# A residual block on one Trainium2 core: the same instructions in another order

## The chip, the core and the metric

The kernel runs on one core of a Trainium2 chip. A core has four compute engines with a queue of instructions each: TensorE (PE, matrix products; its weight loads are shown as PEld), VectorE (DVE), ScalarE (ACT) and GpSimd (POOL). SyncE (SP) issues most DMA transfers, POOL the rest. Each engine works through its own queue in order; between engines, semaphores say when an operand is ready or a buffer is free. The metric is the device time of one execution in microseconds (us), lower is better.

## The reference

```
B, C, HW, E = 2, 512, 64, 1152
def gn(z, gamma, beta):              # group norm, 4 groups, eps 1e-5
    zr = z.reshape(B, G, (C // G) * H * W)
    mu = zr.mean(-1).reshape(B, G, 1)
    var = ((zr - mu) ** 2).mean(-1).reshape(B, G, 1)
    zn = ((zr - mu) / jnp.sqrt(var + eps)).reshape(B, C, H, W)
    return zn * gamma.reshape(1, C, 1, 1) + beta.reshape(1, C, 1, 1)
def conv3(z, w):                     # 3x3 convolution, zero padding, 512 to 512 channels
    zp = jnp.pad(z, ((0, 0), (0, 0), (1, 1), (1, 1)))
    taps = [jnp.einsum("bchw,oc->bohw", zp[:, :, i:i+H, j:j+W], w[:, :, i, j]) for i in range(3) for j in range(3)]
    ...
h = conv3(_silu(gn(x, g1, be1)), w1)
emb = _silu(t_emb) @ w_emb
h = h + emb.reshape(B, C, 1, 1)
h = conv3(_silu(gn(h, g2, be2)), w2)
return x + h
```

Two images of 512 channels and 64 x 64 points pass through two 3x3 convolutions, each behind a group norm and a SiLU, with an embedding added between them and the input added at the end. Inputs and output are bfloat16.

## The kernel before

The work is cut into eight **chunks** c = 0 to 7: layer (0 to 3 the first convolution, 4 to 7 the second), image, and half of the image's rows. In each chunk there are four **units** k = 0 to 3, one for each 128 output channels. The four tiles of 128 input channels are called ct. One partition holds one channel.

The convolution is not computed as nine products. VectorE and ScalarE first combine the rows of the input (and, in the later chunks, its columns) into a few sums, so that fewer products are needed; TensorE multiplies these with combined weights; then the products are combined back into output rows. Per chunk and input tile, `prod(c, ct)` does the first part: `load_a` loads a slab of x or of the stored intermediate h_scr, `silu` applies the norm's scale and shift and the SiLU on ScalarE, `rows_a` and `rows_b` make the row combinations, mostly on VectorE. Per chunk and output tile, `unit(c, k)` does the rest: groups of matmuls into PSUM banks, an evacuation of each bank by ScalarE, and then additions on VectorE that give the output rows in a buffer `ys`. `prod(c+1, k)` is written into the program next to `unit(c, k)`, so VectorE prepares the next chunk while TensorE multiplies this one.

Weights are prepared as well: `prep_w1` combines the first layer's weights on VectorE with scaling passes on ScalarE (128x1536), `prep_w2` does so for the second layer piece by piece (two loads and two 128x384 scaling passes for each of 16 pieces, called w2_jc below), stores them to DRAM, and `fetch_w2` brings them back in chunk 3. `stats0` and `stats1` compute the first norm's statistics, `gn2` the second's. `emb` multiplies the embedding in five short groups of products. At the start TensorE runs 11 + 8 filler products with a matrix of ones ("warm", "fill").

Names in the text are those that the code gives its operations. u63y is unit 3 of chunk 6, the addition "y" that completes the rows; u63m0 is an evacuation of that unit; silu22, k22, row22, rob22 belong to chunk 2 and input tile 2. "k" is a multiplication by 4 of the slab (line 352 on VectorE, 371 on ScalarE), "row" and "rob" are additions (line 348).

**What sets the order.** The code is written as a plan: every operation is recorded in a list, 2,753 of them (1,208 groups of products for TensorE, 821 VectorE, 428 ScalarE, 33 POOL, 263 DMAs), each with its reads and writes in one large SBUF buffer `ar` (addresses fixed by hand) and in PSUM. From these the plan derives which operation must follow which. At the end `emit` issues them in the order that a string, ORDER, spells out: two characters for each operation, a number in base 64.

```
seq = [64 * al.index(order[i]) + al.index(order[i + 1]) for i in range(0, len(order), 2)]
assert sorted(seq) == list(range(len(self.ops)))
done = set()
for i in seq:
    assert all(p in done for p in self.ops[i].preds)
    done.add(i)
    self.ops[i].fn()
```

So ORDER is the only thing that decides how operations stand behind each other in the five queues (PE, DVE, ACT, POOL, SP). Each helper records its operations on one line: additions on VectorE at line 348 (`tt`), multiplications at 352 (`ts`), everything on ScalarE at 371 (`act`), DMAs at 386 (`dma`), products at 401 (`mm`), clearing on POOL at 390. In the profile, lines therefore tell the kind of an operation, and its place in time tells which it is.

Buffers are shared tightly. The two buffers for second-layer weights (RAW) lie in memory that the statistics of the second image use before; an operation that overwrites a buffer waits for its last reader, whichever engine that is on.

Of the kernel before, what the change touches and what calls it, by code (L numbers as in the profile page):

```python
# [115 lines left out]
def _idx(off, dims):  # L116
# [49 lines left out]


ORDER = (
    "0D0E0F0G0H0I0R0S0T0U0W2T1u0v0y1Q2J1N2c3F1r2M0c0X0a0Z0Y0d0e0f00010b020g13030h14150i0j0k0l0L0m170n0N16180405061907"
    "081X1Y1Z1A1_0o1a1c0K1B0M1C1D0p0O1E1b1F1d0q0r1e0s1f0_1g1G1H2021231I1h090A0B0V0C3K1i0J22240t0u0w250x0z1j1J2610271k"  # L170
    "2e12281K292U1l2A1T2B1m1n112C1o2D1x2E2F1U2G1y2P1z1-1W0-1L1M1O1P1R1S1p1q1s1t1v1w2H2I2K2L2N2O3C3D3E3L0Q2Q1V2R2S0P3M"
    "4g2W2l2X2m2Y2n3G2Z4T3g4L2f3O2i3P3N3Q2h3S3R2g3V2a3H3a3W3U2o2p3h3i2q2r2s2t2u2v2w2x2y2z3j2-3u4M2d2j4N2k2_304U2b3Z32"
    "314O5P3X3k3c3d3b5H3Y3T4h4P5I4Q5J4k4V334X4W4Y344Z35364b374a3e4S4R3f384d4m4e4n4f6Y4j3v3w3x3y3z3-3_4243443l45464748"
    "494q4r4s4t3m41404B5Q4A6L4i4c5K6D5L5M6F6M6E4u4v3n3o4w4x4-4_50515253543p555c5d5e5f5h2V4l6Z5R3r6a5T7u5U5S5V3q5W5X7v"
    "5Z5a4p3s5N4C3t3I4D4G4F4E7w4H5b8y4o3J56395Y6GB7B84I3A4z574y3B6IB96H5g586N596P5B5C6O5A6Q5D6RBB6T6SBABD6U6K6W6J6X8z"
    "5O6V5i5j5k5l5m5n5o5r5s5t5u5w5x5y5z5-5_60616b6c6d6e6g5v5q5p6h6i6j6k6l6m6n6s6t6u6v6x6y6z6-6_70717262767763BC4JBN7h"
    "BF6fBP4KBH648-65A0686766BJA169A2BR5E8lBOBGBED56A5F6w7P78797A6o7B7C7D7x7y7z7-5G6p8081BQ828384858687BI74737EDDB47Q"
    "6q7RB57S6r7T7UB67V757W7XBL7FD7DF7YBK7ZBS7aBT7b7G7c7d7H7e7K7f7J7g7i8988D66BDEBM7ID97LDH7j7l8A7m7k7n8B7o7pD27tDL7M"
    "BUEeDN8C8D8EDG7_8F8H8I8J8K8L8M8N8O8S8T8U8V8W8X8Y8Z8_908GD88Q8P91929495969798999A9B9G9H9I9J9L9M9N9O9P9Q9R9S8a9W9X"
    "8m8b7O9p9q6CD37r8RD4DIDB7sDA8cDJ7N7q8d8n8f8p8o8q8g8r8e9C9D8t8s8hDP8v9KEgDKDMDC93DOEfEh9UAt9FEi9EDRDQ9T8x8w9V9Y9Z"  # L180
    "9a9b9c9d9f9eA3A4A5A6A8A9AAABACADAEAFAKALAMANAPAQARASATAUAVAWAaAbAcAdAeAfAgAhEm8u9r9t9s9u9v9w9x8iEuEo9gEjAG9hEqEn"
    "GB9yCrEwA7EpAHAuAO8kEk9k9j9-9i9_9l9zAXCsAYAiAjAvAIAxAwAyAJAzA-A_AZB0B2B3AkCQAlAoAnAmCRCtEvDSEl8jApEO9m9nAqCvB1Cw"
    "CuCxCTCyCzBVBWBXBYBaBbBcBdBZBiGDBjBeBfBgBhBlBmBnBoBtBuBvBwByBzB-B_C0C1C2C3C6C7C8C9CCCDCECFDTDUDVDW9oBkDYDZDaDbBp"
    "BqExBsEbEyEcCUBrEdE-EsErBxEPC5C4AsCAGJCGD0CVCSEzCWCBD1CHC_CIDcDdDeDfDjDkDlCXCYDmDrDsDtDuDwDXDhGLDgDxDyDzD-D_E0E1"
    "E4E5E6E7EAEBECEDF0F1F2F3FxEtE_GCGKDiCKCLG8CJC-G9GFGNCMCZGAArGRCaEQGEESERETGHEUGGEWEVDnDoDvGTGMFyE8E2E3EEGPDpDqCb"
    "EYE9GVHhHUHVGSHjGIEFEJEaCcEGEZEHGOCNCOEXHpHiGQGUF5F6F7F8F9FAFBFCFGFHFIFJFOFPFQFRFTFUFVFWFXFYFDEIGXHlCdGWEKCeFzFE"
    "FKFLF4HrFFHkHxHzFbFZFaFdFcFeFfFgFhFjFkFlFmGZGaGbGcGeGfGgGhGiGjGkGlFSGpGqGrGsGxGyGzG-H0H1H2H3FnH4H5H6H7HqGYHsCPF_"
    "CfG0F-G1CgG3G2ChFMFNCiHtCjFiCkG5FoHvClFpCmG7HmFqFsGmI3FrGuGoGtGnI5J6ELJ7G4HuHnFtG6HyHoI7GvHWKNGdHAHBHCHDHGHHHIHJ"
    "IBICH8ENH9FuI4EMHYHXHZH_HaCnCpHbCoHcGwCqHdHgHfHEG_HFHeHKI6KPJ8J9HwH-KONMNLFvHLIDIEIGIHIIIJIKILIMINIRISITIUIZIaIb"
    "IPIOIFIcIeIfIgIhIiIjIkIlIoIpIqIrIuIvIwIxIQJSJTJUJVJXJYJZJaI8HMIWHPHOIVI0HNI1I9JAHQIXIYImInIsJCJBJDJEItJFJGJJKQIy"  # L190
    "IdIzJHKRI-JKJIJ1IALeLfI2HRJLLgFwMvJ0KTI_KUKSJ2KVKWKXJMNJMwMxHSJWJgJfJbJcJdJeJiJjJkJlJqJrJsJtJmJhO-OzJvJwJxJyJzJ-"
    "J_K0K3JnNKK1K4K5K6K9KAKBKCKjKkKlKmKoKpKqKrKsKtKuKvKzK-K_L0JuK2KbKYLhLiJpJ3KaKZJNJoK7HTKDJ4QBQAOkJOLjLkJPLlLmK8Lo"
    "KELnKnKFKIKGKHLqLpKJKxL1KyKwMyL2MzLsL4L3JQM_KKN0OiOjL5L6L7L8LALBLCLDOxL9LELFLGLHLKLLLMLNLQLRLSLTLOLILJL-L_M0M1M3"
    "M4M5M6M7M8M9MAMEMFMGMHMMMNMOMPMRLUMSMTMUMVMWMXMYMbMcMdMeLPLrLVM-JRLWKcJ5N1M2MDMIMCMBN2LXLYLZN3LaKdKMMJMLMZMaMfN4"
    "N6MKN7MgLbPvRMKLPxRNPwLtOyMQOlMhMiMjMkNNNONPNQNSNTNUMlNVNWNXNYNZNbOHMmOmNRLdKeMnMqOIMoMpKfMrKgMsN5OKOoOLKhOpNaMu"
    "NcNdNeNgNhNiNjNkNlNmNnNrNsNtNuNvNwNxNyN-N_O0O1O2O3O4O5O_P0OqOMKiOnOJLuNoNpOrONP1P2P4NzP5P6P7NfOOOsLvOuNqLwOtPyP3"
    "O6LcSYQ8R7NFR5OPOwO7LxPzSZMtQ9TkR6N8P8P9PAPBPDPEPFPGTlP_R8O8OCPCNHQ0LyO9P-SHNGOBQ1LzRLRKOAPIPJPKPLPMPNPOPPPTPUPV"
    "PWPXPYPZPaPcPdPePfPgPhPiPHPQPjQCQDQEQFQHQIQJQKOvODQ2Q3PSPRPbPkQ4PlN9PmNAPnQLQMQNQOQQQRQSQTQVQWQXQYQZQaQbQcQgQhQP"
    "QiQjQkQlQmQnQpQqQrQsQtR9NBQ7RBRANCOFOEOGSJSIUwUxPpQGPoQUSKSWTTRCTVTUSXNINDRDPqQdQuQvQwRORPRQRRRTRUQ5NEQ6PrPtQoQx"
    "RVRWRXRYRZRaRcRdReRfRhRiRjRkRlRmRnRoPsREQfRFQeRGRHRbSLRJRITiW7SNSMSOSPRgRSQySQQzSRQ-SSSVUfTjUgUhPuRpR1Q_R0SUR2Rs"  # L200
    "RtRuRvRwRxRyRzR_S0S1S2S3S4S5S6SaXJSbS7R-ScSdSfSgShSiSjSkSlSmSoSpSqSrStSuSvSwSxSySzS-OQSTT2T3T4T5T6T7T8R3R4ORRqRr"
    "OSSnS8OTS9OUSAOVOWOXOYOZOaObSDSCSBSEOcOdOeOgS_OfT1OhSeT9TBTCTDTETFTGTHTITmTnToTpTrTsTtTATJTWSsT0TKTLTXTZTMTaTOTb"
    "TNUiTuTvTwTxTyT-T_U0U1U3U4U5U6U7U8U9UAUEUFUGTzUHUIUJUKULUNUOUPUQUBSFTqU2XIUvUuURUSUTUUUyUzU-U_V1V2V3V4V5V6V7V8VA"
    "VBVCVDTYYXSGW6YYVtTPTcTdTQUMVFVGVHVIUVVJVKVLVMVQVRVSVTTeTgUjUDTfUlUCUkUmUnUWThUXUoUpUbUqUYUsVrVsVuV9X1W5TRW4XGX3"
    "X2UaUZVNVvUrVxVwUtUcVyVPYFZnXHZmV0YDVEVUVVVWVXVZVaVbVcVdVeVfVgW8W9WAWBWDWEWFWGWHWIWJWKWMWNWOVYVzVhX4UdTSYEb0a_Ue"
# [12 lines left out]
    "gugtgwgygxg_h0gzg-"
)

@with_exitstack
# [1169 lines left out]
```

## Time and profile before

| what | us |
|---|---|
| median of three runs (460.53 to 462.13) | 461.7 |
| the profiled execution's own time | 461.67 |
| its span, first to last instruction | 459.9 |
| TensorE busy / idle in the span | 445.3 / 14.6 |
| VectorE busy / idle | 440.9 / 19.0 |
| ScalarE busy / idle | 377.3 / 82.6 |
| POOL busy | 65.8 |
| first matmul / first VectorE instruction on x | 1.06 / 4.87 |
| last matmul ends | 454.6 |

The granted TensorE clock is 0.998 on average. The DMA engines move 94.9 MB (206 GB/s over the span); SP issues 213 transfers and POOL 50. A "wait" below is the idle time of an engine in front of an instruction, with the instruction of another engine, or the DMA, that ended it.

### The profile page before, as it was taken

What the parts mean: (1) busy time and instruction counts of PE and PEld (TensorE: products, weight loads), DVE (VectorE), ACT (ScalarE), POOL (GpSimd) and SP (SyncE); (2) the same over time, 40 slices, a digit from 0 to 9 for tenths busy, and PEclk for the clock granted to TensorE, in tenths of its full rate; (3) what the DMA queues carried; (4) which work ended last, traced back from release to release, by engine and by line L of the source; (5) the groups of instructions that cost most, each with busy time, mean ns of one, the idle gap of its engine ahead of it and who ended that gap; (6) DMA issues with size and microseconds to landing.
All of it is one profiled execution on the core that took longest, in us unless ns stands there. A gap on an engine that the chain in (4) does not pass through costs nothing. (4 is left out here: it accounts for less than half of the span.)

```text
span 459.9 us, 8113 instructions
## 1 busy us (share of the span) xinstructions
PE 445.3 (97%) x2891; PEld 280.4 (61%) x2891; DVE 440.9 (96%) x842; ACT 377.3 (82%) x571; POOL 65.8 (14%) x91
## 2 busy tenths in 40 slices
PE   8999999999999899999999999999999999989995
PEld 4744344465555556656666567766776666677882
DVE  4899999989999999999999999999999999999995
ACT  5899999987959899999999898867867889666572
POOL 2210010211011111111000001123103122231210
PEclk9999999999999999999999999999999999999999
DMA  8954682687767487866977697797869988785744
GB/s 319 383 218 152 191 227 72 167 249 213 214 149 232 124 255 205 212 197 193 351 264 261 251 324 198 165 213 204 152 191 254 242 219 209 156 194 115 154 73 93
DMA packets 44472, 94.89 MB, mean 206 GB/s; under 512 B 6544, under 2 KB 18192, under 8 KB 44432
## 3 DMA queue, kind: packets, MB, share of 16 engines
q1 hardware_dynamic: 32208, 77.60, 49.6%
q0 software_dynamic: 11936, 16.78, 23.6%
q8 instruction: 22, 0.36, 0.3%
q14 instruction: 18, 0.15, 0.1%
q10 hardware_dynamic: 288, 0.01, 0.0%
HBM read 62.25 MB, written 31.32 MB: 203 GB/s over the span
## 5 line engine op out<-in xcount | busy, mean ns | idle before, releaser
L401 PE MATMUL psum<-ar 128*128 128x256 f16 (+2 forms) x2771 | 427.7, 316 | 6.8 <-DVE ar L348 4.4
L348 DVE TENSOR_TENSOR ar<-ar 128x1040 f16<-128x1040 f16 (+8 forms) x621 | 409.0, 717 | 7.6 <-ACT ar L371 4.2
L401 PEld LDWEIGHTS <-ar 128*128 128x128 f16 (+1 forms) x2763 | 268.1, 98 | 163.0 <-issue 11.7
L371 ACT ACTIVATE ar<-psum 128x512 f16<-128x512 f32 (+4 forms) x250 | 158.7, 679 | 34.8 <-DVE ar L348 16.4
L371 ACT ACTIVATE ar<-ar 128x512 f16<-128x512 f16 (+6 forms) x146 | 158.9, 1116 | 32.3 <-DVE ar L348 26.0
L371 ACT ACTIVATE ar<-ar,fs 128x2112 f16<-128x2112 bf16 (+1 forms) x32 | 68.8, 2151 | 6.1 <-DVE fs L498 3.0
L386 POOL DMA_DIRECT2D ar<-ar x35 | 38.2, 1111 | 193.0 <-DVE ar L348 78.1
L352 DVE TENSOR_SCALAR ar<-ar 128x512 f16<-128x512 f16 (+3 forms) x90 | 31.5, 370 | 0.4 <-issue 0.2
L386 POOL DMA_DIRECT2D out_dram<-ar x15 | 19.0, 1265 | 52.6 <-DMA ar<-ar 27.2
L371 ACT ACTIVATION_READ_ACCUMULATOR ar<-psum 128x1 f32 x104 | 22.2, 213 | 0.0
L390 POOL MEMSET ar<- 128x65 f16 (+4 forms) x29 | 5.3, 216 | 117.4 <-DVE ar L348 76.8
L401 PEld LDWEIGHTS <-ones_bf 128*128 128x128 bf16 x75 | 7.3, 103 | 6.2 <-issue 3.5
L401 PE MATMUL psum<-ar,ones_bf 128*128 128x260 bf16 x56 | 7.3, 275 | 1.1 <-DMA ar<-in_x_dram 0.9
L401 PE MATMUL psum<-ones_bf 128*128 128x512 bf16 x19 | 6.3, 466 | 1.1 <-DVE ones_bf L405 1.1
L371 ACT ACTIVATION_READ_ACCUMULATOR ar<-ar 128x1 f32 x36 | 7.3, 201 | 0.0
L479 POOL TENSOR_TENSOR fs<-fs 128x1 f32<-128x1 f32 x4 | 3.7, 917 | 18.0 <-DVE fs L477 18.0
L401 PEld LDWEIGHTS psum<-fs,ones_neg 128*128 128x128 f32 x36 | 4.7, 191 | 1.8 <-ACT ar L371 0.9
L401 PE MATMUL psum<-fs,ones_neg 128*128 128x1 f32 (+3 forms) x36 | 4.7, 244 | 0.3 <-ACT ar L371 0.3
L439 ACT ACTIVATE s_sb<-tparm 128x18 bf16<-128x18 bf16 x1 | 0.2, 218 | 3.2 <-DMA tparm<-in_t_emb_dram 3.2
L438 DVE CAST fs<-gparm 128x16 f32<-128x16 bf16 x1 | 0.2, 175 | 2.7 <-DMA gparm<-in_params_dram 2.7
L401 PE MATMUL psum<-ar,s_sb 128*2 128x512 bf16 x9 | 2.7, 377 | 0.0
L433 ACT ACT_TABLE_LOAD x1 | 1.3, 1283 | 1.7 <-PEq L1375 1.7
(54 smaller groups left out, 25.5 us busy)
## 6 DMA issues: line engine op xcount, KB each, us to landing
ar<-in_w_dram SPq DMA_DIRECT2D x36, 384.0 KB, 4.2
ar<-in_x_dram SPq DMA_DIRECT2D x16, 552.5 KB, 4.8
h_scr<-ar SPq DMA_DIRECT2D x16, 520.0 KB, 3.8
ar<-h_scr SPq DMA_DIRECT2D x16, 520.0 KB, 4.4
ar<-ar POOLq DMA_DIRECT2D x31, 260.0 KB, 4.6
out_dram<-in_x_dram SPq DMA_DIRECT2D x30, 260.0 KB, 5.2
out_dram<-ar POOLq DMA_DIRECT2D x15, 520.0 KB, 6.5
ar<-in_x_dram SPq DMA_DIRECT2D x13, 520.0 KB, 4.9
```

The source lines that it names most:

```text
L348: pl.op("DVE", 0.075 + 0.000521 * out.n, lambda: nc.vector.tensor_tensor(out=out.ap, in0=a.ap, in1=b.ap, op=op), regs(a, b), regs(out), name)
L352: pl.op("DVE", cost or 0.075 + 0.00026 * out.n, lambda: nc.vector.tensor_scalar(out=out.ap, in0=a.ap, scalar1=s, scalar2=None, op0=ALU.mul ...
L371: lambda: nc.scalar.activation(out=out.ap, in_=a.ap, func=func, scale=sc, **kw), regs(*rr), regs(*ww), name)
L386: lambda: eng.dma_start(out=out, in_=in_, **kw), regs(*r), regs(*w), name, lat=3.2 if sw else None, after=after, sw=sw, seq=seq)
L390: pl.op("POOL" if eng == "gpsimd" else "DVE", 0.08 + 0.0005 * out.n, lambda: e.memset(out.ap, v), (), regs(out), name)
L401: nc.tensor.matmul(out.ap, lhsT=lhsT.ap, rhs=rhs.ap, start=st, stop=sp, skip_group_check=True)
L433: nc.scalar.activation(out=fs[:, WARM:WARM + 1], in_=fs[:, WARM + 1:WARM + 2], func=ACT.Silu)
L438: nc.vector.tensor_copy(out=fs[:, GB:GB + 4 * CT], in_=gparm[:])
L439: nc.scalar.activation(out=s_sb[:], in_=tparm[:], func=ACT.Silu)
L479: pl.op("POOL", 0.85, lambda: nc.gpsimd.tensor_tensor(out=F(rs, n).ap, in0=N.ap, in1=F(NEGH, n).ap, op=ALU.pow), regs(N), regs(F(rs, n)), ...
```

## The change

Only the string ORDER is replaced. The same 2,753 operations are issued with the same operands and addresses; the derived dependencies are the same, since they follow from the order in which operations are recorded, not issued.

```
 ORDER = (
-    "0D0E0F0G0H0I0R0S0T0U0W2T1u0v0y1Q2J1N2c3F1r2M0c0X0a0Z0Y0d0e0f00010b020g13030h14150i0j0k0l0L0m170n0N16180405061907"
+    "0D0E0F0G0H0I0R0S0T0U0y0v0A2T0C092J1N0c0X0a0Y0Z00010203040506070b0g13080d0e0f0h0i0V2U0j0k0l0m0B3K1415170n1618190K"
...
-    "gugtgwgygxg_h0gzg-"
+    "f-gtgwgxgyg_gzh0g-"
 )
```

What it amounts to, counted in the two built programs:

| | before | after |
|---|---|---|
| matmuls and weight loads, VectorE, ScalarE and POOL instructions, DMAs | the same | the same |
| pairs of neighbours on VectorE of which the second needs the first | 43 | 54 |
| separate wait instructions: PE / DVE / ACT / POOL / SP | 8 / 191 / 163 / 85 / 143 | 12 / 195 / 168 / 86 / 132 |
| filler products in front of the first product with x | 11 + 1 | 11 + 7 |

On TensorE the convolution's groups keep their order; what moves are the fillers, the statistics' products and the five groups of `emb`, which come earlier. On VectorE, ScalarE, SP and POOL operations of neighbouring units and of the next chunk's preparation are interleaved differently all along. From unit u71 on, TensorE's order is the same in both.

More of the change, by code (lines that the diff above doesn't have):

```diff
@@ L174 @@
[L174 to L193, printed above, removed]
@@ new lines @@
+    "0L0o1A0M1B0p1C0r0q1D1E0s1F0_0O101X1Y1Z1b1Q2c2M1r1a1c1G0N11221_201d0t0u210w0x241e121f1g1H1I1h0W3F4T1u3C4g1i23251j"
+    "1J1K1k2627281T1l292A1U2B1m1n1V1o2e2C2D0J2F1x2E1y2G1-1z2P1W3E2d3L2Q0Q2S2R0P3M2f3O2h2g3P3N3D3g0z0-1L1M1O1P1R1S1p1q"
+    "1s1t1v1w2H2I2K2L2N2O2W2X2l2a2Y2Z2m3h4L3i4U4N3H2n2o2p2q2r2s2t2u2v2w2x3j2y2z3G2b4M2V3Q2i3S3J3R3a2j2k3W3X3c3d3U3V3Y"
+    "2_2-3u3v3w3k3l3x3y3z3-3_42434O3T3130324h3m5H443n45464748494q4r4s4t5P3o3Z3p4k4V334X344Y4W37354Z4Q4S364b3b4a3I4P38"
+    "4R3e3f4m4n4f5K6L4c5J5I6D4B5Q41406Y3r5R3q5T5S6Z5U4e6a5M4A6E6F4j5L4u4v4w4x4-4_50513s525354555c5d5e5f5h5i5j5k3t5l5m"
@@ new lines @@
+    "5n5o5r5s5t5u4C5V4d7u5W4D5X4E5Z7v4F4G4l4i7w4H4o39B7B96M3A6G5Y574y8y5b4pBB564z6N5a6O6P586Q5C6R596T5B5A3BB8BA6H4I5g"
+    "6I6S5D6U6JBD6W6VBN8l6XBC6K5O8zBP5w5x5y5z5-5_60616b6c6d6e5v6g6h6i6j6k6l6m6n6s5p6t6u6v6x6y6z6-63626fBR5q8-64A06865"
+    "A15N66674KA26_7071726w7677787PBGBF4J69BHBJBO5EBQ6o6p797A7B7C7D7x7y7z7-80818283745G7E73BI6qDDBEBT7h5F6AD5DFD77FBS"
+    "6BDE7Q7RB47S7TB57UB67V7W7X6r7YBL7Z757aBK7b7G7c7d7H7e7K7f7J7g7ID97L7iDH7j7l7k7mD6BMBUD27nD37o7p8m7_DG88DIDJ7r8485"
+    "8687898C8D8E8F8H8I8J8K8L8M8N8O8S8T8U8V8W8X8Y8Z8_909192948PD88G9596978Q8a8b7qDLDN9pEeEg6C8BD48A7sDB8R7tDADMEfEh7M"
```

66 lines of the change are left out of this document (38 added, 28 removed).

## The prediction

> **What bounds the kernel now.** I read first the page's totals, then who waits for whom on TensorE and VectorE, then the chain that ended last, and last the timeline around VectorE's longest waits.
>
> ```profile
> span 459.9 us, 8113 instructions
> PE 445.3 (97%) x2891; PEld 280.4 (61%) x2891; DVE 440.9 (96%) x842; ACT 377.3 (82%) x571; POOL 65.8 (14%) x91
> PE 6%; DVE 2%; ACT 0%; issue 0%; DVEq 0%; ACTq 0%
> L348 DVE TENSOR_TENSOR ar<-ar 128x1040 f16<-128x1040 f16 (+8 forms) x621 | 409.0, 717 | 7.6 <-ACT ar L371 4.2
> ```
>
> Two engines are full at once: TensorE (PE) is idle 14.6 us of 459.9 and VectorE (DVE) 19.0 us. A new order adds no work, so all that it can win is idle time; the chain on the page covers only the last tenth of the span and does not say which of the two engines set the pace before. The waits do:
>
> ```profile
> PE psum L401 <- DVE ar L348: 4.4, 7, 1.6
> PE psum L401 <- ACT ar L371: 1.5, 4, 0.7
> DVE ar L348 <- ACT ar L371: 4.2, 4, 2.0
> ```
>
> TensorE waits mostly for VectorE (4.4 us, seven times). VectorE's long waits are few, so what VectorE has queued ahead of the instruction that TensorE wants is what sets the time. The chain, in order of time, shows the last such meeting:
>
> ```profile
> 416.58 3.44 DVE ar L348 x6
> 420.11 1.03 ACT ar L371
> 421.18 28.12 PE psum L401 x256
> 450.44 1.24 DVE ar L348
> ```
>
> The six DVE instructions end with u63y (418.81 to 420.01; the name as in the code: unit of chunk 6, k 3, its add "y"). ScalarE then evacuates u70's bank and TensorE runs u71 to u73 without a gap for 28.12 us. In the new order TensorE's last 136 blocks, from u71 on, stand exactly as before, so **the end moves by what u63y moves**, unless a new wait arises behind it. Where VectorE lost time before u63y:
>
> ```profile
> 17.56 0.29 DVE L1194 SCALAR_TENSOR_TENSOR ar<-psum,ident 128x128 bf16<-128x128 f32 x1 [0.63 <-ACT ar L371]
> ...
> 77.40 0.69 DVE L348 TENSOR_TENSOR ar<-ar 128x1024 f16<-128x1024 f16 x1 [0.33 <-PE psum L401]
> ...
> 83.65 0.69 DVE L348 TENSOR_TENSOR ar<-ar 128x1024 f16<-128x1024 f16 x1 [0.58 <-ACT ar L371]
> ...
> 98.49 0.52 ACT L371 ACTIVATE ar<-ar 128x384 bf16<-128x384 bf16 x1 [1.88 <-DMA ar<-in_w_dram]
> ...
> 99.04 1.16 DVE L348 TENSOR_TENSOR ar<-ar 128x768 f16<-128x768 bf16 x2 [1.33 <-ACT ar L371]
> ...
> 151.38 0.60 PE L401 MATMUL psum<-ar 128*128 128x512 f16 x2 [1.61 <-DVE ar L348]
> ```
>
> Brackets give the idle time in front and its releaser. The wait at 99.04 is a late weight load, passed on by ScalarE; TensorE pays at 151.38, where chunk 2 opens and VectorE is not ready.
>
> **The change, part by part.** All durations stay; I add them up in both orders.
>
> *Added: neighbours that depend on each other.* In the trace, a VectorE instruction that does not need the one just before starts 0.081 us before that one's end (median of 777 pairs); one that needs it starts 0.035 us after (43 pairs). A dependent pair thus costs 0.116 us. The new order has 54 such pairs instead of 43. Ahead of u63y stand the same number of instructions in both orders, 756, with 25 dependent pairs before and 33 now: 8 x 0.116 = **+0.93 us**. Summed in the same way, VectorE has more ahead at the earlier meetings too: +0.45 us at u20 (151.38), +0.57 (168.6), +0.70 (274.1), +0.81 (309.5), +2.06 at u60 (360.0; one 1.23 us add, u52y, now stands in front as well), +1.20 at u70 (409.9).
>
> *Removed: VectorE's waits.* At 77.40 the add u01s waits for TensorE's last product with w_emb; that block moves forward by 6.0 us of TensorE work, u01s by less, so the distance grows by 1.1 us. At 83.65 u02s waits for ScalarE's evacuations of u02, which now lie 2.4 us further ahead of it. At 99.04 the w2 row add waits for ScalarE's scaling pass and its load; it now stands 2.9 us later against that pass, and another block's weights (w2_02) are taken first. Each wait also loses the 0.081 us of overlap: 0.41 + 0.66 + 1.41 = **-2.48 us**. For each, between nothing (another wait in its place) and the whole; I take the whole, since the shift is larger than the wait in all three.
>
> *The head.* At 17.56 VectorE waits 0.63 us (0.71 with the overlap). In the new order the first chunk's row operations stand in front of that instruction, but TensorE's small product with ones_neg for channel tile 2 needs its result, and the first convolution blocks stand behind that product. Worth 0 to 0.71; I take the middle, **-0.35**. Seven of TensorE's eight filler blocks (512 columns, 0.215 us apart) now run before the first x arrives: 4.85 + 7 x 0.215 = 6.35 against the 6.17 at which that block starts now. ScalarE's square pass (1.92 us, to 8.39) covers the 0.18 us; without that cover it would cost 0.18.
>
> *Moved: loads, stores and passes.* SP's queue still issues 213 DMAs, POOL's 50; SP's separate wait instructions fall from 143 to 132, VectorE's rise from 191 to 195, ScalarE's from 163 to 168, TensorE's from 8 to 12. No row shows such an instruction's cost. At four places (291.5, 303.8, 365.3, 380.7) a VectorE instruction starts some 0.19 us late although the ScalarE pass that it needs ended 0.8 to 3.8 us earlier, and at most of the others nothing is lost: four more cost 0 to 0.8 us. I take 0, as most rows show none.
> The move that worries me is on ScalarE near 122 us. The scaling pass w2_12 (second load) now stands in front of u12's first evacuation, one square pass and silu22; in the old order silu22 came first. Its load is issued when VectorE has finished the w2_03 adds: 121.81 + 1.28 (more ahead) - 2.83 (waits gone) = 120.3, plus 0.5 for the load in front, 120.8. In the profile the same load was used 4.7 us after its issue; the median of its kind is 4.2, and the latest, the one behind the wait at 98.49, took 7.7. From the pass to the end of silu22 is 5.8 us of ScalarE work (start-to-start times of the same passes), so silu22 ends at 131.3 (4.7), 130.8 (4.2) or 134.3 (7.7). k22 on VectorE wants it at 134.31 - 0.21 - 2.83 = 131.3. The cost is 0, 0 or 3.0; I take 0, by the same load's own time.
>
> *TensorE's own waits* (0.56 us at 90.55, 0.83 at 356.27, 0.24 at 381.41, all behind ScalarE) shrink, since the passes wanted are 1.4, 3.1 and 3.7 us further forward. This wins nothing by itself: it lets TensorE follow VectorE. At u60 VectorE is only 0.8 us earlier (2.83 - 2.06), so TensorE waits there anew, yet it still waited 1.2 us at 409.85 and has that to give.
>
> *Sum.* 461.67 (the profiled execution: span 459.9 and 1.8 around it; the median of the three runs is 461.7) + 0.93 - 2.48 - 0.35 = **459.8 us**.
>
> The Trainium skill, "VectorE: DVE Perf Modes", section "The DRAIN you can't avoid", says the flush after each VectorE instruction comes whether or not the next one waits ("the semaphore costs nothing extra here"). By that rule the pair term is 0 and the sum would be 458.8. The trace disagrees (0.035 against -0.081 us), so I keep the row.
>
> **Rivals.**
> 1. *The idle time moves, it does not go.* VectorE meets as much waiting elsewhere, and only the pairs are left: 461.67 + 0.93 = 462.6. For it: 82% busy ScalarE is reordered throughout, and its passes stand nearer to their inputs at 128 us. Against it: at every place where VectorE waited for ScalarE, the distance in queue work has grown.
> 2. *Slower: silu22 late behind the w2_12 load.* With the 7.7 us lateness, and nothing won in the head: 461.67 + 0.93 - 2.48 + 3.0 = 463.1. Up to a lateness of 4.7 us nothing is lost; from about 6.3 the gain is gone, then the time grows one for one, since u20 finds VectorE with no slack (0.05 us at 151.38). For it: that lateness happened at 98.49. Against it: the load's neighbours in SP's queue near 121 us are those of the old order, and there it took 4.7 at most.
> 3. *Dependent pairs cost nothing.* If the 0.116 us were hidden in waits that were due anyway, 461.67 - 2.83 = 458.8. Against it: in long stretches VectorE does not wait at all (0.17 us of idle at 100 to 120, 0.07 at 160 to 180). The section of the Trainium skill named above would make it so.
>
> **How the numbers follow.** 0.3% (1.4 us) is about what can be told from no change here; faster means under 460.3, slower over 463.1. Forecast 0.40 (0.35 faster, 0.05 within); rival 1 0.22 (0.17 within, 0.05 slower, if the extra wait instructions cost their 0.8); rival 2 0.29 (0.24 slower, 0.05 within); rival 3 0.09, faster. Faster 0.44, within 0.27, slower 0.29. The low end, 457.8, is rival 3 with the whole of the head (-0.36) and some 0.6 of the small 0.19 us delays gone; the high end, 464.5, is rival 2 with one more wait of 1.4 like that at 99.04. The likeliest case alone holds 458.8 to 460.7: the head whole or none (0.35), the wait instructions 0 to 0.6, the pairs at half their cost.
>
> **What would show it.** Right: no VectorE wait over 0.3 us between 60 and 110; TensorE's 1.61 us wait at u20 gone; a wait of about 1 us before u60; the last uninterrupted TensorE stretch of 28.1 us starting near 419.3. Wrong: a ScalarE wait on in_w near 122 followed by a VectorE wait at k22 near 131; VectorE idle in sum not smaller than 19.0; or a wait inside TensorE's last stretch, which I take to be unchanged.

## The result and the profile after

| | median us (lowest to highest) | ratio to before, 95% interval |
|---|---|---|
| before, beside it | 461.35 (460.53 to 462.13, 4 runs) | |
| after | 467.55 (466.39 to 470.08, 4 runs) | 1.0143 [1.0104, 1.0182] |

The new order is slower by 6.2 us; forecast was 459.8, and the range ended at 464.5. The profiled execution took 467.67 us, 6.0 more than the one before. The page's totals of the changed kernel, span and busy time of each engine:

```profile
span 465.9 us, 8116 instructions
PE 446.3 (96%) x2891; PEld 280.6 (60%) x2891; DVE 442.2 (95%) x842; ACT 376.1 (81%) x571; POOL 66.4 (14%) x91
```

The work is the same; the idle time is not. VectorE is idle for 465.9 - 442.2 = 23.7 us instead of 19.0, TensorE for 19.6 instead of 14.6. Who waits for whom (total, times, longest):

```profile
PE psum L401 <- DVE ar L348: 6.7, 9, 3.5
PE psum L401 <- ACT ar L371: 4.6, 5, 1.7
...
DVE ar L352 <- ACT ar L371: 4.3, 2, 2.7
DVE ar L348 <- ACT ar L371: 3.0, 5, 1.0
...
DVE ar L352 <- issue: 1.0, 1, 1.0
```

New is VectorE at line 352, the "k" multiplications: before, no wait of theirs was on the list beyond one of 0.2. The chain that ended last, start and length:

```profile
422.19 1.31 DVE ar L348 x3
423.50 0.05 issue
423.55 31.74 PE psum L401 x287
...
455.37 1.03 ACT ar L371
...
456.43 1.24 DVE ar L348
```

The end is as before, only later: the ScalarE pass and the addition behind TensorE's last stretch come at 455.37 and 456.43 instead of 449.39 and 450.44. u63y ends at 426.00 instead of 420.01, so the shift of the whole program, 5.99 us, is there at u63y, as the prediction had it. Where VectorE and TensorE lost it, from the timelines:

```profile
25.06 0.29 DVE L1194 SCALAR_TENSOR_TENSOR ar<-psum,ident 128x128 bf16<-128x128 f32 x1 [0.75 <-ACT ar L371]
...
69.39 0.73 DVE L352 TENSOR_SCALAR ar<-ar 128x2145 f16<-128x2145 f16 x1 [1.66 <-ACT ar L371]
...
148.45 0.72 DVE L352 TENSOR_SCALAR ar<-ar 128x2145 f16<-128x2145 f16 x1 [2.69 <-ACT ar L371]
...
154.96 1.26 PE L401 MATMUL psum<-ar 128*128 128x512 f16 x7 [3.48 <-DVE ar L348]
...
203.17 1.44 DVE L348 TENSOR_TENSOR ar<-ar 128x1040 f16<-128x1040 f16 x2 [0.54 <-ACT ar L371]
...
346.81 0.72 DVE L352 TENSOR_SCALAR ar<-ar 128x2145 f16<-128x2145 f16 x1 [1.05 <-issue]
...
366.72 1.05 PE L401 MATMUL psum<-ar 128*128 128x512 f16 x5 [1.29 <-DVE ar L348]
```

These are k12 (69.39), k23 (148.45), u20 on TensorE (154.96), row33 (203.17), k62 (346.81) and u60 (366.72). An account of u63y follows from the end of each VectorE instruction minus the sum of what stands ahead of it in the queue (durations and neighbour gaps as in the prediction); what is left over is idle time:

| VectorE, us | before | after | difference |
|---|---|---|---|
| queue ahead of u63y | 408.36 | 409.29 | +0.93 |
| idle up to the last statistics instruction (26 and 29 us) | 4.44 | 5.50 | +1.06 |
| idle from there to u20 (151 and 155 us) | 3.90 | 5.97 | +2.07 |
| idle from there to u60 (360 and 367 us) | 3.01 | 4.67 | +1.66 |
| idle from there to u63y | 0.30 | 0.57 | +0.27 |
| end of u63y | 420.01 | 426.00 | +5.99 |

The three waits at 77.40, 83.65 and 99.04 are gone: between 70 and 148 us VectorE has no wait over 0.3. In their place stand 1.66 at k12 and 2.69 at k23. For both, the page names ScalarE, but silu12 ended at 67.72, 1.67 us ahead of k12, and silu23 at 144.63, 3.8 us ahead of k23. There is one more operand. In chunks 1 to 3, line 721 of the code adds two planes of a tile's row sums (260 KB) onto two others by a DMA on POOL's queue, called va and the chunk and tile, instead of by a VectorE addition. The next tile's k writes into the buffer that this DMA reads. So k12 waits for va11, which landed at 62.61 + 6.70 = 69.31 (k12 started at 69.39), and k23 for va22. The queues of SP and POOL around va22 (POOL's instruction is va22):

```profile
138.25 0.33 SPq L386 DMA_DIRECT2D u_scr<-ar  x1
138.68 1.57 SPq L386 DMA_DIRECT2D h_scr<-ar  x1
140.34 0.38 SPq L386 DMA_DIRECT2D ar<-in_x_dram  x1
140.78 0.85 SPq L386 DMA_DIRECT2D ar<-in_w_dram  x1
140.87 0.92 POOL L386 DMA_DIRECT2D ar<-ar  x1 [5.35 <-PE psum L401]
141.71 0.43 SPq L386 DMA_DIRECT2D h_scr<-ar  x1
```

and that one DMA by the tile it writes, POOL's instruction alone:

```profile
L386 POOL DMA_DIRECT2D ar<-ar x1: 916/916/916, 140.9 to 140.9; - x1
DMA to landing us min/median/max: 7.5/7.5/7.5
```

va22 landed at 140.87 + 7.50 = 148.37, and k23 started at 148.45. What the DMA engines moved in the first 3.9 us behind its issue (140.87 to 144.80), by queue, in packets, MB and share of the 16 DMA engines' time; SP's transfers are q1, and q0, POOL's, has no packet yet:

```profile
q1 hardware_dynamic: 262, 0.98, 96.3%
```

In the kernel before, va22 took 3.6 us (issued at 139.46), and k23 started at 145.09 with nothing to wait for.

### The profile page after: what moved, and what is told of

Same layout as the page of the kernel before. It is cut to its first block, busy times and chain, and to the rows that moved or that the text cites. A ratio compares the mean times of both kernels' runs of the same rounds, so it can differ in the third digit from the quotient of the medians.

```text
span 465.9 us, 8116 instructions
## 1 busy us (share of the span) xinstructions
PE 446.3 (96%) x2891; PEld 280.6 (60%) x2891; DVE 442.2 (95%) x842; ACT 376.1 (81%) x571; POOL 66.4 (14%) x91
## 3 DMA queue, kind: packets, MB, share of 16 engines
q0 software_dynamic: 11936, 16.78, 23.7%
## 5 line engine op out<-in xcount | busy, mean ns | idle before, releaser
L348 DVE TENSOR_TENSOR ar<-ar 128x1040 f16<-128x1040 f16 (+9 forms) x621 | 409.0, 719 | 5.7 <-ACT ar L371 3.0
L386 POOL DMA_DIRECT2D out_dram<-ar x15 | 18.0, 1202 | 81.5 <-DMA ar<-ar 58.8
L371 ACT ACTIVATION_READ_ACCUMULATOR ar<-psum 128x1 f32 x104 | 23.8, 229 | 0.0
L390 POOL MEMSET ar<- 128x65 f16 (+4 forms) x29 | 7.2, 277 | 102.4 <-DVE ar L348 63.6
```

The costliest lines, as they stand in the source:

```text
L348: pl.op("DVE", 0.075 + 0.000521 * out.n, lambda: nc.vector.tensor_tensor(out=out.ap, in0=a.ap, in1=b.ap, op=op), regs(a, b), regs(out), name)
L371: lambda: nc.scalar.activation(out=out.ap, in_=a.ap, func=func, scale=sc, **kw), regs(*rr), regs(*ww), name)
L386: lambda: eng.dma_start(out=out, in_=in_, **kw), regs(*r), regs(*w), name, lat=3.2 if sw else None, after=after, sw=sw, seq=seq)
L390: pl.op("POOL" if eng == "gpsimd" else "DVE", 0.08 + 0.0005 * out.n, lambda: e.memset(out.ap, v), (), regs(out), name)
```

## The experiments

All are orders of the same 2,753 operations. "va landing" is the time from POOL's issue to the DMA's last semaphore event. The times:

| kernel | median us (lowest to highest) | ratio to before, 95% interval |
|---|---|---|
| e1_fill | 467.96 (466.29 to 470.06) | 1.0156 [1.0123, 1.0188] |
| e2_va22 | 466.52 (464.62 to 467.78) | 1.0122 [1.0088, 1.0156] |
| e3_va11 | 466.69 (465.07 to 467.50) | 1.0121 [1.0098, 1.0145] |
| e4_a62 | 466.96 (465.64 to 470.18) | 1.0142 [1.0098, 1.0185] |
| s1_bu20a | 462.98 (461.37 to 463.73) | 1.0051 [1.0034, 1.0068] |
| s2_au20b | 466.96 (463.92 to 468.76) | 1.0125 [1.0082, 1.0169] |
| s3_bab | 467.64 (466.58 to 468.75) | 1.0147 [1.0125, 1.0169] |
| e5_fixes | 463.16 (461.71 to 465.47) | 1.0046 [1.0022, 1.0070] |
| b_fix | 460.74 (460.39 to 461.11) | 1.0000 [0.9991, 1.0008] |
| b_a30 | 460.64 (460.11 to 461.54) | 1.0000 [0.9991, 1.0009] |
| f1_sp | 467.53 (465.49 to 469.57) | 1.0138 [1.0106, 1.0170] |
| f2_cover | 467.05 (464.78 to 468.13) | 1.0111 [1.0085, 1.0138] |
| e6_more | 462.83 (461.14 to 464.24) | 1.0031 [1.0017, 1.0046] |
| e7_row32 | 462.27 (461.37 to 463.18) | 1.0025 [1.0015, 1.0036] |

The kernel before had medians of 460.7 to 461.2 beside them.

### One repair at a time

**e1_fill**, TensorE's queue alone:

```diff
-warm fill1 fill2 fill3 fill4 fill5 fill6 fill7 st00 st01 fill8 st00 st01 st01 st01
+warm fill1 st00 fill2 st01 fill3 st00 st01 st01 fill4 fill5 fill6 st01 fill7 fill8
```

> The changed kernel with filler products 2 to 8 put back between the statistics' products, as in the kernel before; only TensorE's queue differs. Theory (fillers in front of the first x cost what the slow clock makes of them): the first product with x starts within 0.1 us of the DMA's landing (6.2 instead of 7.46), VectorE's wait at the first statistics falls from 2.66 to about 2.0, and its idle time up to 30 us falls from 5.5 to about 4.4: the end moves by -1.1, 466.4. Rival (the head's idle time is swallowed by the wait of 1.66 us at k12 near 69, which is set by a DMA): the first product moves, but VectorE's idle time in front of u20 stays the same and the time stays at 467.5.

The first product with x started at 5.97, and VectorE's first wait fell as expected. It came back 15 us later (VectorE's timeline):

```profile
25.03 0.29 DVE L1194 SCALAR_TENSOR_TENSOR ar<-psum,ident 128x128 bf16<-128x128 f32 x1 [1.39 <-ACT ar L371]
```

1.39 instead of 0.75 at the same instruction (statistics tile 3). It starts 0.12 us behind the end of ScalarE's pass on the same product, in e1_fill as in the profile of after. That pass starts at 24.5 us in both, 22.0 before, but not for the same reason. In the profile of after TensorE's last product of tile 3 ended at 23.85, and the pass stood behind another pass of ScalarE. In e1_fill ScalarE is 0.67 us earlier (its pass for tile 2 starts at 19.56 instead of 20.23; before, at 17.05) and then waits 0.52 us for that product, which in the new order stands behind two convolution groups and ends at 24.48 (20.84 before): its eight parts took 1.94 us instead of 1.06. In this execution the granted TensorE clock was at half just there (PEclk, the third number from the right):

```profile
core 0: us, PE busy (x) PEld busy (x) DVE busy (x) ACT busy (x) POOL busy (x), PEclk, DMA share, GB/s
21.65:25.04 3.39, 3.39 (x13) 1.81 (x12) 1.93 (x7) 2.82 (x5) 1.23 (x2) 0.50 1.04 405
```

VectorE's idle time up to there is 5.26 us against 5.29 in the profile of after. So the run does not tell what the fillers cost: what it gained at the first wait was lost to the clock of this execution, and its time does not differ from that of after. What it does show is that the statistics of tile 2 come 2.5 us later on ScalarE in the new order, even with the fillers put back.

**e2_va22**, VectorE between k22 and u12d, and one store:

```diff
 VectorE
-k22 w2_12 row22 row22 rob22 w2_12 u12S rob22 u12S rob22 rob22 u12A rob22 u12s
+k22 u12S row22 row22 rob22 u12S rob22 u12A rob22 rob22 rob22 w2_12 u12s w2_12
 SP
-a23 w2_10 w2_11 w2_13 w2_13 w2_20 w2_12 u10st a30
+a23 w2_10 u10st w2_11 w2_13 w2_13 w2_20 w2_12 a30
```

> The changed kernel with thirteen VectorE operations between k22 and u12d permuted so that va22 is issued about 1.1 us earlier and the load a30 some 2 us behind it instead of 0.5 us ahead; the store u10st is taken out of the neighbourhood. Theory (va22 lands late, 7.5 us, because a30 and the stores share the DMA engines with it): it lands within 4.5 us, k23 no longer waits (2.69 us gone), TensorE's 3.65 us wait at u20 falls to about 1, and the end moves by -2.7: 464.9. Rival (the accumulating DMA is late by itself): it still takes over 7 us, k23 waits some 1.6 us, -1.1: 466.4. Second rival (k23 waits for silu23 on ScalarE, as the page names it): nothing changes, 467.5.

VectorE's timeline (k22 and k23) and the issues of va22 and a30:

```profile
135.31 0.73 DVE L352 TENSOR_SCALAR ar<-ar 128x2145 f16<-128x2145 f16 x1 [1.55 <-ACT ar L371]
...
141.37 0.92 POOL L386 DMA_DIRECT2D ar<-ar  x1 [6.68 <-PE psum L401]
...
143.43 0.40 SPq L386 DMA_DIRECT2D ar<-in_x_dram  x1
...
146.63 0.72 DVE L352 TENSOR_SCALAR ar<-ar 128x2145 f16<-128x2145 f16 x1
```

```profile
L386 POOL DMA_DIRECT2D ar<-ar x1: 916/916/916, 141.4 to 141.4; - x1
DMA to landing us min/median/max: 3.4/3.4/3.4
```

va22 landed in 3.4 us and k23 did not wait: the theory's mechanism, and not ScalarE. But with the store u10st 1.6 us ahead of it, va21 landed in 6.1 us instead of 4.1 to 4.2 (every other run with this neighbourhood), and k22 waited 1.55. The late transfer was moved, and with it the wait.

**e3_va11**, SP's queue:

```diff
-st12  a13  st13
+st12  st13  a13
```

> The changed kernel with one load, a13 (552 KB), issued behind st13 instead of 1.2 us ahead of the accumulating DMA va11. Theory (neighbours make it late): va11 lands in 5 us instead of 6.7, k12's wait of 1.66 us near 69 goes, and the end moves by -1.7: 465.9. Rival (neighbours in the queue do not matter, or the time comes back at the next wait): the time stays at 467.5, with the wait at k12 still there or one of 1.5 us between 70 and 100.

va11 landed in 5.5 us and k12 waited 0.45. This shows nothing: e1_fill and s2_au20b, with a13 where the changed order has it, had va11 in 5.6 and 5.5 us and waits of about the same size, e4_a62 in 7.4 us with a wait of 2.4. The spread from run to run is wider than the effect.

**e4_a62**, POOL's queue (a62 is the clearing for that load):

```diff
-u43oa  u43out  u50oa  a62
+u43oa  a62  u43out  u50oa
```

> The changed kernel with POOL's clearing for a62 in front of the store u43out, behind which and behind u50oa it stands there. Theory (the load a62 is late since its clearing stands behind two POOL instructions that wait for VectorE): a62 is issued about 3.9 us earlier, ScalarE's wait of 3.8 us for h_scr goes, so do k62's wait of 1.14 us at 346.8 and TensorE's 1.35 us at 349.2: -1.1, 466.4. Rival (the time comes back at the wait before u60, 1.45 us at 366.7): TensorE's wait there grows by as much and the time stays at 467.5.

The load was issued 2.7 us earlier, ScalarE's wait for it fell from 3.8 to 1.0, and k62 did not wait any more. But k62 did not wait in e2_va22 and f2_cover either, where the clearing stands as in the changed order and the load landed in 6.3 us instead of 7.3 to 7.5. So k62 waits for this load; that its clearing stands late is one part of it, and how long it takes is another. The time did not show the repair: in that execution k12 had already waited 2.4 us.

### Which part of the order loses

**s1_bu20a**, **s2_au20b** and **s3_bab** join the two orders at seams:

```diff
-ORDER = after
+ORDER = before up to rob23 (opens u20), after for the rest                    # s1_bu20a
+ORDER = after up to rob23, before for the rest                                # s2_au20b
+ORDER = before up to k12, after up to silu22, before for the rest             # s3_bab
```

> Order of the kernel before up to rob23, the VectorE instruction that opens u20 for TensorE (near 151 us), and the changed order for all the rest. Theory (each part of the order carries its own waits, and they add): rob23 ends at 151.3 as before; from there to u63y the changed order has 265.9 us of queue and 5.2 us of idle time of its own, so u63y ends near 422.4 and the time is 464.0. Rival (the whole loss lies in the first third, and the waits of the rest, at row33 and k62, are there only because VectorE came in late): 461.4. Second rival (the time that the first part wins comes back in later waits, as with the single repairs): 466 to 467.5.

> The reverse: the changed order up to rob23, the order before for the rest. Theory (the parts add): rob23 ends at 154.9, then 265.4 us of queue and 3.3 us of idle time: u63y near 423.6, the time 465.0. Rival (whole loss in the first third): 465.0 too, with s1_bu20a at 461.4; the two are told apart by that one. Second rival (the order before has slack behind u20 that takes up a late start): 461.4 to 463.

> The order before up to k12 (69 us), the changed order from there to silu22 (ScalarE, near 131 us), the order before for the rest; the store u10st, which falls at the seam, stands behind the w2_13 loads (near 132 us). So it has the part in which the three waits of before (77.40, 83.65, 99.04) vanish, without the changed head and without the changed place of va11 and va22. Theory (the three waits were worth their length, and it was the neighbourhood of the accumulating DMAs that took it back): those waits gone, 0.6 us of dependent pairs added, u63y 1.9 us earlier: 459.5. Rival (what is won in front of k22 is lost at k22 or k23, because the accumulating DMAs va21 and va22 do not land earlier): a VectorE wait of 1 to 2 us at 134 or 145 and 461.4.

By their medians s1 and s2 add up, as the theory has it: 0.51% behind u20 and 1.25% ahead of it, against 1.43% [1.04, 1.82] for the whole. But s2's runs are not alike: 463.92 at a granted clock of 0.997, and 466.16 to 468.76 at 0.987 to 0.989. Part of its 1.25% thus goes with a lower clock, and the split is rough. s3 was a misfit of mine: the seam left SP's last load for `emb` in its late place while VectorE wanted its result early, and VectorE waited 2.4 us at 72.5 and 1.7 at 77.6 for it. It tells nothing of the question it was made for.

A by-product of s1 matters more. Up to u20 it has the order before, yet two of the waits that I had counted were missing: u01s did not wait, and the w2_01 load, which took 7.7 us in the profile of before, landed in 6.4 and held nobody up; in b_a30, again with that order, in 6.3. The 1.33 us at 99.04 was that one execution's.

### The repairs together, and the old waits by themselves

**e5_fixes**:

```diff
-ORDER = after
+ORDER = before up to 26 us, after for the rest, with e3_va11's a13, e4_a62's a62, e2_va22's VectorE order
+        and u10st behind the w2_20 load near 133 us
```

> The changed kernel with four repairs at once: the order before up to 26 us (fillers, statistics), a13 behind st13, va22 ahead of a30 (with u10st near 133 us, away from va21 and from va22), and a62's clearing in front of u43out. Theory (waits of the changed order, each worth its length): 0.9 (head), 1.2 (k12), 2.7 (k23), 1.1 (k62) off 467.5: 461.6, with the waits at row32 and row33 (0.5 and 0.6) left. Rival (half of each comes back at the next late transfer or ScalarE pass, as e1_fill, e2_va22, e3_va11 and e4_a62 showed for one at a time): 464.5, with longer waits at row32 and row33.

467.55 - 463.16 = 4.4 us of the 6.2 came back. rob23, which opens u20, ended at 150.25, exactly where it ended in s1_bu20a with the order before. va22 landed in 3.4 us, va21 in 4.2, and va11 in 4.0, as in e6_more and in no other profile; why is open.

**b_fix**: the order before, with the waits that the prediction removed filled with ready work, and nothing else.

```diff
-st01  st02  st01  row00  row00
+st01  row00  st02  st01  row00
-st12  u01s  emb  st10  u01d  u014  u012  u018  n1_1  u01y  rob12
+st12  st10  n1_1  u01s  emb  u01d  u014  u012  u018  rob12  u01y
-st10  u02s  k13  u02d  row13
+st10  k13  u02s  row13  u02d
-u038  w2_01  n1_3  u03y
+u038  n1_3  u03y  w2_01
```

> The kernel before with four small permutations on VectorE alone, one at each of the waits that the prediction counted as gain: row00 in front of the statistics' instruction at 17.56 (0.63 us), n1_1 in front of u01s at 77.40 (0.33), k13 in front of u02s at 83.65 (0.58), n1_3 and u03y in front of the w2_01 row add at 99.04 (1.33, which in the profile of s1_bu20a, with the same order up to there, was not there). The cover of the accumulating DMAs stays at 8 and 6 us of VectorE work. Theory (a wait is worth its length as long as no cover of a DMA is shortened): 0.71 + 0.41 + 0.66, one dependent pair more (0.12), and the w2_01 load's lateness in some runs: 461.1 - 1.7 = 459.4, with no VectorE wait over 0.3 us between 15 and 110 except behind a DMA. Rival (VectorE only reaches the next meeting earlier and waits there): one new wait of 1 us or more before 151 us and 461.1.

Nothing: 1.0000. VectorE's timeline shows why:

```profile
17.65 0.29 DVE L1194 SCALAR_TENSOR_TENSOR ar<-psum,ident 128x128 bf16<-128x128 f32 x1
...
18.87 0.16 DVE L469 COPY fs<-psum 128x2 f32<-128x2 f32 x1 [0.17 <-PE psum L401]
...
23.61 0.16 DVE L469 COPY fs<-psum 128x2 f32<-128x2 f32 x1 [0.34 <-PE psum L401]
...
83.73 1.31 DVE L348 TENSOR_TENSOR ar<-ar 128x1024 f16<-128x1024 f16 x2 [0.29 <-ACT ar L371]
...
91.03 1.17 DVE L348 TENSOR_TENSOR ar<-ar 128x768 f16<-128x768 f16 x2 [0.41 <-ACT ar L371]
```

The wait at 17.56 is gone, and VectorE stands at 18.87 and 23.61 instead, waiting for TensorE's next statistics products; the one at u01s is gone, and VectorE waits at 83.73 and 91.03 for ScalarE. Up to u20 its idle time is 7.22 us, against 7.12 in b_a30, whose VectorE order is that of before. TensorE and ScalarE set the time at which these results exist; VectorE, early, waits one meeting later.

### Cover or neighbours

The stretch of VectorE work between the last instruction that an accumulating DMA needs and the k that waits for it (its cover), summed from the queues, and the landings in the profiles (s3_bab and the repaired places left out):

| | cover before | cover after | landing, order of before around it | landing, changed order around it |
|---|---|---|---|---|
| va10 to k11 | 8.2 | 6.4 | 4.3 to 4.5 | 4.5 to 5.0 |
| va11 to k12 | 8.1 | 5.7 | 6.1 to 7.7 | 5.5 to 7.4 |
| va21 to k22 | 6.1 | 5.1 | 4.2 | 4.1 to 4.2 |
| va22 to k23 | 6.1 | 5.4 | 3.6 | 6.4 to 7.5 |
| va32 to k33 (ScalarE) | | | 3.9 | 6.1 to 8.1 |

(POOL issues some 0.6 us after the last input, so a landing of cover minus 0.6 is just hidden.) The waits follow the landings closely. In the eight profiles with the changed order of VectorE around k12 in which va11 took over 5 us, the wait at k12 is that time minus 5.03 to 5.04 us (5.48 gives 0.45, 7.39 gives 2.36); in the six with the changed order around k23, the wait there is the time of va22 minus 4.80 to 4.81 (6.41 gives 1.60, 7.50 gives 2.69). So these two waits are for these two DMAs. But two things changed, the cover and the landing, and three runs part them.

**b_a30**: the order before, SP issues a30 and u11st some 2 us ahead of va22.

```diff
-w2_13  w2_21  a30  w2_20  w2_11  w2_12  u11st
+w2_13  a30  u11st  w2_21  w2_20  w2_11  w2_12
```

> The kernel before with one change in SP's queue: the load a30 (552 KB) and the store u11st (520 KB) some 2 us ahead of the accumulating DMA va22 instead of 2 to 4 us behind it. VectorE's order, and with it the cover of 6.1 us, is that of before. Theory (neighbours on the DMA engines make the accumulating DMA late, over 6.5 us instead of 3.6): k23 waits 1 to 1.9 us near 145 (before: none), TensorE's wait at u20 grows by as much, the time is 462.1 to 463. Rival (it is only the shorter cover on VectorE that made k23 wait): no wait at k23, 461.1.

k23 without a wait, and va22's landing:

```profile
143.87 0.71 DVE L352 TENSOR_SCALAR ar<-ar 128x2145 f16<-128x2145 f16 x1
```

```profile
L386 POOL DMA_DIRECT2D ar<-ar x1: 916/916/916, 138.2 to 138.2; - x1
DMA to landing us min/median/max: 4.6/4.6/4.6
```

One microsecond later than undisturbed, which the cover of 6.1 hides: two large transfers 2 us ahead are not enough.

**f1_sp**: the changed kernel, SP's queue alone.

```diff
-w2_20  w2_12  u10st  a30
+w2_20  u10st  w2_12  a30
```

> The changed kernel with one DMA moved in SP's queue: the store u10st (520 KB) behind the w2_20 load near 133 us instead of 2.2 us ahead of va22. VectorE's order, and with it the cover of 5.3 us of work between va22 and k23, stays. Theory (va22 is late for the bytes in flight around it; it landed in 3.4 to 4.6 us with up to 1.1 MB near it and in 6.4 to 7.5 with 2.1 MB): it lands in 5 to 6 us, k23 waits 0 to 0.8 us instead of 1.7 to 2.8, and the time is 465 to 466. Rival (it is VectorE's shorter cover): the wait stays at 1.7 to 2.8 us and the time at 467.5.

k23 and va22's landing:

```profile
148.11 0.72 DVE L352 TENSOR_SCALAR ar<-ar 128x2145 f16<-128x2145 f16 x1 [1.86 <-ACT ar L371]
```

```profile
L386 POOL DMA_DIRECT2D ar<-ar x1: 916/916/916, 141.4 to 141.4; - x1
DMA to landing us min/median/max: 6.7/6.7/6.7
```

So it is not u10st either, and my count of bytes in flight falls. In f1_sp four SP issues (the store of w2_12, 384 KB; a30; the load w2_20, 96 KB; u11st) come 2.6, 2.2, 1.7 and 0.5 us ahead of va22; in e2_va22 the same four come 1.6 to 3.4 us behind it: 6.7 against 3.4 us. Shown is that va22 is late behind that group and early ahead of it. The traces' packet records also show where the time goes. Ahead of the group (e2_va22) and in the kernel before, the first packet of va22 starts 1.5 us after its issue; in f1_sp it starts 2.6 us after it, in the profile of after 4.0, and until then the DMA engines move SP's packets alone (0.96 and 0.98 MB). In all of them va22 lands 0.3 to 0.4 us after its last packet started. So its packets wait for their turn; which transfer of the group costs most is open.

**f2_cover**: the changed kernel, VectorE alone.

```diff
-emb  k12  emb  row12  row12  n1_0  rob12  rob11  n1_0  emb  u01s  rob12  rob11
+emb  emb  n1_0  rob11  k12  rob11  row12  row12  rob12  n1_0  emb  u01s  rob12
-u12y  k23  u13S  row23  row23  rob23  u13S  rob23  n1_2
+u12y  u13S  n1_2  k23  u13S  row23  row23  rob23  rob23
```

> The changed kernel with VectorE's order alone changed at two places, DMAs as they are: four ready operations (emb, n1_0, rob11 twice) in front of k12, so that the cover of va11 is 7.5 us of work instead of 5.7 (before: 8.1), and two (u13S, n1_2) in front of k23, so that that of va22 is 6.1 instead of 5.3 (before: 6.1). 0.35 us of dependent pairs are added. Theory (the cover decides at k12, where va11 takes 6 to 7.7 us in both orders; the bytes in flight decide at k23): k12 waits 0 to 0.3 us instead of 0.5 to 2.5; k23 still waits 0.9 to 2; the time is 466 to 466.8. Rival (traffic decides at both): k12's wait stays at over 1 us, since the transfer is later.

k12 and k23:

```profile
69.95 0.72 DVE L352 TENSOR_SCALAR ar<-ar 128x2145 f16<-128x2145 f16 x1 [0.16 <-issue]
...
147.66 0.72 DVE L352 TENSOR_SCALAR ar<-ar 128x2145 f16<-128x2145 f16 x1 [1.82 <-DMA ar<-ar]
```

As the theory has it at both places. At k12 the cover decides: va11 landed in 7.0 us here, late as ever, and with 7.5 us of cover k12 waited 0.16. At k23 a cover as long as before does not help against a landing of 7.5. In this run the page names the accumulating DMA itself as the releaser. The time stayed at 467: what k12 did not wait was lost near 190 and 205 us, where row32 waited 1.5 and row33 1.3, as against 0.4 and 0.54 in the profile of after. (In this execution the granted clock was 0.50 from 153.5 to 156.9, behind TensorE's wait for u20; what that added is not shown.)

### The rest of the loss

**e6_more**: e5_fixes with u21st away from va32, three ScalarE passes ahead of two evacuations, and the second st_3 load earlier.

```diff
 SP
-a40  u21st  w2_32  a40  w2_33  w2_30
+a40  w2_32  a40  w2_33  w2_30  u21st
-a73  pre71  u73x  pre71  st_3
+a73  st_3  pre71  u73x  pre71
 ScalarE
-u61o4  u604  u61o5  u602  u608
+u604  u602  u608  u61o4  u61o5
```

> The repaired kernel e5_fixes with three more repairs in the second part: the store u21st (520 KB) behind the w2_30 store near 196 us instead of 0.8 us ahead of the accumulating DMA va32; on ScalarE the three passes u604, u602, u608 in front of the evacuations u61o4 and u61o5, which wait for the accumulating DMA u53oa; the second st_3 load behind a73 instead of behind two stores that wait for TensorE. Theory (what is left of the loss, 2 us, is late transfers again): the waits at row33 (0.47) and u60y (1.78) go, 463.2 - 2 = 461.2, level with the kernel before. Rival (VectorE's waits only move to the next meeting, as in b_fix): 463.2.

**e7_row32**: e6_more, and on ScalarE

```diff
-w2_23  k32
+k32  w2_23
```

> e6_more with one pair exchanged in ScalarE's queue: k32 in front of the w2_23 scaling pass, which waits 1.6 us for its weight load and holds k32 up behind it. VectorE's wait at row32 was 1.03 us in e6_more, the last one over 0.5 us between 25 and 430. Theory (this wait is the rest of the loss): k32 starts near 180.3 instead of 182.3, row32 waits no more, and the time falls by 1.0, to 461.8. Rival (by now VectorE's waits move only to the next meeting, as in b_fix): one or two new waits before 280, 1 us in sum, and 462.8.

In e5_fixes u60y waited at 383.88 (its passes stood behind an evacuation that waits for the accumulating DMA u53oa, 9.2 us after that one's issue):

```profile
383.88 2.47 DVE L348 TENSOR_TENSOR ar<-ar 128x2048 f16<-128x2048 f16 x3 [1.69 <-ACT ar L371]
```

and in e6_more VectorE runs through:

```profile
381.47 4.85 DVE L348 TENSOR_TENSOR ar<-ar 128x2048 f16<-128x2048 f16 x6
```

The wait at row33 is gone too. Over all profiles with the changed order there, that wait follows the landing of va32: none up to 6.2 us, 0.4 at 6.75, 0.54 at 7.1, 1.3 to 1.7 at 7.7 to 8.1. In e6_more va32 landed in 5.5; whether the moved u21st did that is not shown, since e2_va22 and e4_a62, without the move, had 6.1 and no wait. In e7_row32 the wait at row32 is gone; 0.60 us of it come back at 189.09, at the w2_30 row add. The medians fall to 462.83 and 462.27. That is less than expected, and the intervals of e5_fixes, e6_more and e7_row32 overlap. In e7_row32 u63y ends at 420.00: the queue ahead of it is 409.06 us and the idle time 10.95, against 408.36 and 10.37 in b_a30 and 408.48 and 10.79 in b_fix. The repaired order thus has about VectorE's idle time of the order before, plus 0.6 to 0.7 us of dependent pairs, and is 1.1 us slower (462.27 against 461.16).

No order beat the kernel before.

## Why the prediction was wrong

*The end moves by what u63y moves.* Right: 5.99 us at u63y, and the whole program is 6.00 longer. TensorE's last stretch had no wait, as predicted.

*Added: +0.93 for dependent pairs.* Nothing speaks against it: the gaps have the same medians in the profile of after (0.034 us behind, 0.084 us ahead), the account closes with it, and the repaired order is left with its share of it. The rule that I set beside it (the Trainium skill, "VectorE: DVE Perf Modes", "The DRAIN you can't avoid": a semaphore costs nothing extra) is not borne out here.

*Removed: -2.48 for three waits, taken whole.* **This step was sized too large.** The waits vanished as said, and in the profile of after that shows as far as k22: between the starts of k12 and k22 VectorE is idle for 65.10 - 64.59 = 0.51 us, before for 65.71 - 63.20 = 2.51. But over half of the sum, 1.41, was one execution's late load, absent in the two other profiles with that order there; in one of them, b_a30, the same stretch has 1.30 us of idle time, so some 0.8 was there to win. And won in front of k22 is not won at the end: b_fix removes the waits alone and gains 0.0% (interval within 0.1%), since VectorE waits at the next meeting instead. The prediction had a rival that says this ("the idle time moves, it does not go", 462.6) and gave it 0.22. The repaired order came close to that number (462.3), but it is not the order that was forecast.

*The head, -0.35.* Wrong in sign: +1.06 us of idle. The wait at 17.56 went, but the statistics of the last two channel tiles come later on ScalarE and TensorE, and VectorE waits for them at 25.06. Fillers: the first x product came 1.29 us later and not 0.18, since the clock in that execution came up only at 6.16 us (3.98 in the profile of before). The filler interval of 0.215 us that I used holds only behind that point. In the seven profiles with these fillers in front, that product starts between 6.54 and 7.71. What this costs in the end is open, since e1_fill lost its gain to a halved clock.

*What was not in the sum.* **The step that failed most is the term "Moved: loads, stores and passes", which was put at 0: no cover of a transfer was compared between the two orders, except for w2_12.** The prediction said that "at every place where VectorE waited for ScalarE, the distance in queue work has grown". It did not look at the places where VectorE did not wait because a DMA was well covered. There the distances shrank, 8.1 to 5.7 us for va11 (shown to decide by f2_cover), and SP issues a store and a load ahead of va22 that stood behind it before (e2_va22 against f1_sp shows that the group in which they stand decides). That cost 1.66 + 2.69 us in the profiled run. The rest lies behind u20: row32 with 0.40 behind a scaling pass that waits for its load (e7_row32), row33 with 0.54 behind va32, k62 with 1.05 behind the load a62. These five waits are 6.3 us that the sum did not have; in the profile before, VectorE waits at none of the five places. u60y behind u53oa is no part of it: in the profile of after u60y does not wait.

*The rival "silu22 late behind the w2_12 load".* Its place was wrong: the load was issued at 123.89 instead of 120.8 and landed in 2.4 us, ScalarE waited 1.77 for it, silu22 ended at 132.19, and k22 at 134.49 did not wait. Its kind was right: a late transfer in front of u20, which finds VectorE with no slack.

*u60.* The wait forecast there, about 1 us, is there with 1.29.

## What to carry to other kernels

A wait in one trace is neither a standing one nor worth its length: look at it in several executions, and fill it with ready work alone before counting it. When an order changes, compare for every transfer how much work lies between its issue and its user, also where nothing waits now, and what is issued in the two microseconds ahead of it. A releaser named by the page that had ended microseconds before is a sign of another operand, here both times a DMA. Read the granted clock of an execution before comparing its time with another's.

## What the runs showed of the hardware

The same accumulating DMA of 260 KB, va22, landed in 3.4 to 3.6 us ahead of SP's large transfers and in 6.4 to 7.5 behind them. The Trainium skill, "DMA: Bandwidth & Descriptors", section "Queues, rings and completion order", states that a semaphore increment lands only after every earlier write of that DMA engine, whichever queue it came from. That alone does not make va22 late here: its packets themselves started late (4.0 us after the issue instead of 1.5), it landed 0.3 to 0.4 us after the last of them started, early or late, and in the profile of after every SP transfer issued ahead of it had landed by 146.09, 2.3 us before it. The profiles of va22 thus do not show a semaphore held back by this rule. Behind two transfers 2 us old (b_a30) va22 took 4.6 us. By the fit in the Trainium skill, "DMA: Bandwidth & Descriptors", section "Anatomy of one DMA — SWDGE (gpsimd) path", a transfer of 260 KB would take 2.0 + 0.6 = 2.6 us, an estimate; the section does not say whether its fit holds for a DMA that adds, and no run had less than 3.35 for va22.

The same transfer in the same order spreads: va11 5.5 to 7.4 us in six profiles with the changed order around it. The changed kernel's own times spread as well, 466.4 to 470.1, while the kernel before stayed within 460.3 to 462.9 in all series.

The granted TensorE clock spreads too, and I had overlooked it. The kernel before has 0.996 to 1.000 in every run beside the experiments; of the changed kernel's four runs the slowest (470.08) has 0.990, the others 0.996 to 0.998. In seven profiles (e1_fill, e2_va22, e4_a62, s3_bab, e5_fixes, f1_sp, f2_cover) the clock stands at 0.50 for one or two stretches of 3.4 us inside the program, each beginning between 0.3 us before and 1.6 us after the end of a TensorE wait of 1.3 to 3.5 us. Such a wait does not always bring it: the profile of after has one of 3.48 at u20 and no such stretch, so its 6 us of loss are not this. At half the clock, a stretch of 3.4 us takes up to 1.7 us of TensorE's work, an estimate; two of them, as in the profiles of e2_va22 and f1_sp, which also have a granted clock of 0.990, would make most of the 2.4 to 3.7 us between the slowest run and the others. That the waits cause the drops is likely but not tested.

TensorE's fillers were 0.43 us apart at first and 0.215 later; the change came 2.9 us after the first one in the profile of before and 5.1 in that of after, with the same eleven fillers in front.
